# Moving 128 value loads from SyncE's to GpSimd's queue, with a new step order, in a local attention and MLP kernel

## The chip, the cores and the metric

The kernel runs on one core of a Trainium2 chip. The metric is the device time of one execution in microseconds (us). Before the change, three runs took 199.34, 200.52 and 202.75 us; the median is 200.52. Names of engines: PE is TensorE, DVE is VectorE, ACT is ScalarE, POOL is GpSimd, SP is SyncE. SP computes nothing; its queue issues DMA transfers. POOL computes a little and can issue transfers too.

## The reference

The input `x` has 2048 rows (positions) of 512. It is normalised by rows, and the result `xn` goes through two branches that are multiplied and, with `x`, make the output `x + s * g`, in the kernel's terms.

```python
xn = _layernorm(x)
# branch A: local attention, 32 heads of 16, 8 keys per query at distance 0, 2, ... 14
q, k, v = split(xn @ wqkv)
idx = pos[:, None] - off[None, :]          # off = 0, 2, ..., 14
logits = einsum("bhsd,bhswd->bhsw", q, k[idx]) * scale
logits = where(idx >= 0, logits, -1e9)     # the mask: only the first 14 rows have it
s = einsum("bhsw,bhswd->bhsd", softmax(logits), v[idx]) @ wo
# branch B: a shifted mixer and an MLP
h  = gelu(_layernorm(xn) @ w1)
x1 = xn + shift_groups(h) @ w2             # four groups of columns, shifted by 1, -1, 2, -2 rows
g  = silu(x1 + gelu(_layernorm(x1) @ w3) @ w4)
return x + s * g
```

## The kernel before, in words

The 2048 rows are 16 tiles of 128 rows, in 4 chunks of 4 tiles. The kernel defines named steps (functions that issue a few instructions) and then runs through one written list, `ORDER`, that calls each step once. An engine executes its own instructions in that order and each instruction waits for its inputs, so the list fixes five queues, one per engine, that proceed at their own pace. The number in a name is a tile (0 to 15) or a chunk (0 to 3); `lv3.0` is part 0 of the load of tile 3, `qk1.2` part 2 of chunk 1.

The steps that the change and the prediction touch:

- `x0`..`x3`, `xc1`..`xc3` load `x`. `st` (L262) takes the statistics on DVE; `rsa`, `rsb`, `rsc`, `r2a`, `r2b` turn them into scales (`rsb` L275 and `r2b` L297 on POOL); `xn` normalises (L304 on DVE in chunk 0, L308 on ACT after it).
- `tr0`..`tr3` (L329) transpose the tiles of chunk 0 on PE into one PSUM tile of two banks, `xe0`..`xe3` (L334) copy them out on ACT. Chunk 1 is transposed by PE and copied by DVE (`tr1.0`, `xe1.0`), chunks 2 and 3 by DMA from SP (`tx`, L339).
- `qk` (L393) makes eight blocks of q and k for a chunk, `qe` (L399) copies them out on ACT. `v` and `h` (L405) make the values and the mixer's input for one tile; `ve` (L411) copies the values to an SBUF tile of which there are three, and `vst` (L416) stores them to DRAM from POOL's queue. `he` (L420) applies the gelu on ACT, `hst` (L426) transposes by DMA from SP into `hT`.
- `pw` (L448) multiplies q with shifted k on DVE, `lg` (L457) sums over each head on PE. For chunk 0 `mask` (L464) writes -1e9 into the logits. Then `mx`, `ls`, `to`, `sh` (DVE) and `ex` (ACT) make the softmax of a chunk, `et` (L506) transposes it on PE, `ae` (L512) copies it out.
- `lv` (L655) loads the eight shifted copies of the values of a tile back from DRAM into one of three `vs` buffers, four DMAs per step. `pr` (L661) multiplies them by the weights in place on DVE, `ws` (L670) sums on PE, `oe` (L676) copies out, `oTe` transposes (by DMA from SP, L690; for the last three tiles by PE in `ot`), `wo` (L715) multiplies by the output weights. A `vs` buffer is free again when its `ws` is done.
- `mix` (L553) is the shifted product with `w2`: it needs the `hT` of its own tile and of its neighbours, and at the ends of a chunk the columns that `pl` and `pr_` (L540, L547) copy on POOL. `xo` (L559), `s3` (L562), `ra3`, `rb3` (L571, POOL), `rc3`, `xm` (L580, ACT) normalise; `x1T` (L586) transposes by DMA from SP; `w3` (L608), `ge` (L615), `w4` (L623), `yy` (L629), `si` (L632) are the MLP; `sg` (L720), `fa` (L723) and `out` (L727) combine and store.

Every DMA of this kernel waits, besides its data, for the transfer eight places before it on the same kind of queue, since eight semaphores go round. Matmul results go through six PSUM buffers; a matmul step waits until the step six places before it has been copied out.

Of the kernel before, what the change touches and what calls it, by code (L numbers as in the profile page):

```python
# [16 lines left out]
warm0 sel x1 qa0 x0 x2 w1 x3 root wqk0 wqk1 st0 wv st1 xc1 rsa0 w2 xn0 rsa1 st2 tr0 xe0 xn1 rsa2 st3 wo.0 h0  # L17
xn2 rsa3 tr1 xn3 tr2 xe1 xe2 tr3 r2a0 h1 xe3 r2q0 h2 r2b0 he0 h3 v0 he2 hst0 qk0.6 ve0 st6 he1 qk0.0 vst0 w3.1
st7 qe0.6 pl0 hst1 v2 qe0.0 st4 qk0.3 ve2 st5 hst2 vst2 he3 rsa1.0 qe0.3 rsb1.0 lv0.0 v1 qk0.5 ve1 rsc1.0 r2a1
xn6 qk0.2 vst1 hst3 qe0.5 r2b1 qk0.1 xn4 xc3 qe0.2 mix1 lv0.1 qe0.1 qk0.7 xn5 xo1 xn7 qk0.4 s31 xc2 qe0.7  # L20
tr1.0 qe0.4 lv1.0 tr1.1 xe1.0 mix0 qa1 pw0.0 h4 xe1.1 lv1.1 v5 he4 xo0 qk1.2 st12 ve5 qk1.7 vst5 s30 hst4
qe1.2 st11 lg0.0 qe1.7 qk1.0 lv2.0 pl1 st8 h7 qe1.0 st10 qk1.4 w4.1 he7 st9 qk1.5 lv2.1 pw0.2 qe1.4 pr_0 h5
qe1.5 rsa2.0 st14 rsb2.0 qk1.6 he5 hst7 st15 v3 qe1.6 rsc2.0 hst5 st13 xn8 mix2 r2a2 ve3 v4 tx8 rsa3.0 xn10
r2b2 pw0.1 mix3 xn9 tx10 xo2 rsb3.0 ve4 v7 xo3 xn11 qk1.1 vst4 s32 tx9 ve7 vst3 rsc3.0 qk1.3 r2a3 qe1.1 vst7
w3.0 s33 xn15 lg0.2 r2b3 tx11 lg0.1 pw0.7 qe1.3 h6 xn12 mix4 ra30 he6 pw0.5 rb30 xn13 h8 hst6 xo4 xn14 v8 rc30
s34 he8 v6 xm2 hst8 h10 ve8 ve6 vst8 tx12 lg0.7 xm0 lg0.5 vst6 pw0.4 v10 he10 pl2 x1T0 xm3 h9 pw0.6 ve10 pr_1
tx13 h11 he9 vst10 lg0.6 he11 lg0.4 tx15 mix5 pw0.3 mix7 x1T2 pw1.0 qa2 v11 tx14 xo7 qk2.7 ve11 xo5 w3.3 qk2.1
vst11 s37 qe2.7 w3.2 v13 s35 qe2.1 hst10 xm1 qk2.3 ve13 x1T3 lg0.3 qe2.3 qk2.2 vst13 mask x1T1 qk2.4 pw1.1
qe2.2 v9 hst11 qe2.4 mx0 mix6 ve9 hst9 ls0 v12 vst9 h14 w4.2 xo6 ve12 ex0 s36 qk2.5 vst12 h12 ra31 rb31 v14
he14 to0 w4.0 lg1.0 h15 rc31 sh0 w30.7 qe2.5 he12 qk2.0 ve14 hst12 he15 pw1.2 w30.4 vst14 ge0.7 pl3 hst14 et0  # L30
qe2.0 pr_3 w30.5 ge0.4 ae0 xm5 hst15 w30.9 pr0 ge0.5 w30.1 xm4 pr_2 ge0.9 qk2.6 x1T4 ge0.1 pr1 xm7 ws0 x1T5
lg1.2 qe2.6 lg1.1 w30.10 oe0 lv3.0 pw1.5 v15 ge0.10 w30.8 pw1.3 ve15 x1T7 w30.3 vst15 ge0.8 pr2 xm6 lg1.3
lg1.5 lv3.1 ge0.3 w30.2 w30.6 ge0.2 pw1.4 x1T6 w30.0 ge0.6 pw1.7 ws2 ge0.0 oTe0 lg1.4 oe2 ws1 pw1.6 lg1.7 w42
lv4.0 pw2.4 qa3 pr3 oTe2 qk3.6 oe1 oTe1 w41 qe3.6 yy2 lv4.1 si2 ws3 yy1 lg1.6 w40 oe3 lv5.0 mx1 si1 pw2.0 oTe3
ls1 mix9 lv5.1 qk3.5 xo9 ex1 yy0 mix10 s39 mix8 lv6.0 xo10 qk3.7 qe3.5 xo8 si0 to1 qk3.4 lv6.1 w31.2 s38 qe3.7
w43 qe3.4 sh1 ge1.2 s310 qk3.1 yy3 et1 qe3.1 w31.8 ae1 si3 w31.6 pr4 w31.4 ge1.8 w31.10 pr5 wo.3 mix11 wo.2
ge1.10 w31.9 ge1.4 ge1.6 w31.7 xo11 ge1.9 wo.1 pr6 ws5 ge1.7 lg2.0 oe5 ws4 lg2.4 oe4 lv7.0 w31.3 pw2.1 wo1
ge1.3 pw2.3 wo0 lv7.1 w31.5 sg1 s311 w31.1 ge1.5 oTe5 fa1 wo2 ra32 ge1.1 sg0 rb32 lv8.0 lg2.3 sg2 lg2.1 w31.0
pw2.6 qk3.0 ge1.0 out1 rc32 pw2.5 oTe4 xm8 h13 qe3.0 pr7 w45 xm11 x1T8 he13 xm9 lv8.1 fa0 wo3 fa2 yy5 lg2.5
x1T9 sg3 si5 lg2.6 qk3.3 pw2.2 hst13 w47 pw2.7 qe3.3 xm10 x1T11 fa3 lg2.2 out3 yy7 lg2.7 out2 ws7 out0 mx2 si7  # L40
ws6 x1T10 qk3.2 oe7 oe6 ls2 w44 oTe7 qe3.2 pw3.2 ex2 oTe6 pw3.0 w46 lv9.0 yy4 to2 si4 lv9.1 mix12 yy6 w32.5
sh2 si6 mix14 lv10.0 ge2.5 w32.8 xo12 xo14 et2 ge2.8 lv10.1 w32.1 s312 ae2 w32.10 ge2.1 s314 mix15 ge2.10 pr8
w32.6 mix13 ge2.6 w32.7 xo15 xo13 wo6 ge2.7 s315 wo5 s313 w32.0 sg5 lg3.0 ra33 sg6 ge2.0 ws8 rb33 lg3.2 pr10
oe8 lv11.0 w32.2 w32.4 ge2.2 w32.9 oTe8 rc33 ge2.4 pr9 xm12 w32.3 lv11.1 ge2.9 wo7 xm14 pw3.4 wo4 ge2.3 xm13
x1T12 w411 sg7 sg4 x1T14 pw3.5 x1T13 ws10 fa5 yy11 lg3.5 oe10 lg3.4 w48 pr11 si11 out5 oTe10 xm15 pw3.7 w49
x1T15 yy8 pw3.1 si8 lg3.7 fa4 ws9 pw3.6 out4 lg3.1 oe9 w410 lv12.0 fa7 pw3.3 oTe9 yy9 lg3.6 yy10 lg3.3 si9
# [10 lines left out]
def kernel(  # L57
# [202 lines left out]
    def plan_ln1(c, t, dk):  # L260
# [63 lines left out]
        def tr1(i):  # L324
            if i == 0:
                ps["tr0"] = ps_lg.tile([P, 2, 2, ND, P], BF16, name="tr0_ps", tag="lg")
            pt = ps["tr0"][:, i % 2, i // 2, :, :]
            for dt in range(ND):
                nc.tensor.transpose(pt[:, dt, :], xn_t[i][:, dt * P : (dt + 1) * P], ident[:])  # L329

        def xe1(i):
            if i == 0:
                xnT_t[0] = xnTp.tile([P, ND, CH], BF16, name="xnT", tag="xnT")
            nc.scalar.activation(xnT_t[0][:, :, i * P : (i + 1) * P], ps["tr0"][:, i % 2, i // 2, :, :], AF.Copy)  # L334
# [311 lines left out]
    def plan_attend(i, t, tw):  # L646
        c, jj = i // TPC, i % TPC

        def load_vs(uh):
            if uh == 0:  # L650
                vs_t[i] = vsp.tile([P, NB, 2, D], BF16, name="vs", tag="vs")
            vs = vs_t[i]
            for u in range(U4 * uh, U4 * uh + U4):
# [1 line left out]
                nc.sync.dma_start(  # L655
                    out=vs[T32 * (u % U4) : T32 * (u % U4) + T32, :, u // U4, :],
                    in_=v_dram[r0 : r0 + P, :].rearrange("(b t) d -> t b d", t=T32))
# [142 lines left out]
```

## Time and profile before

| what | value |
|---|---|
| median of 3 runs | 200.52 us |
| the profiled execution | 202.74 us |
| its span, first to last instruction | 201.0 us |
| mean granted PE clock | 0.989 |
| PE busy | 187.4 us, 93% |
| DVE busy | 165.6 us, 82% |
| ACT busy | 132.5 us, 66% |
| POOL busy | 30.8 us, 15% |
| transfers on SP's queue (q1) | 33.24 MB, 67.8% of the 16 DMA engines' span |
| transfers on POOL's queue (q0) | 2.11 MB, 3.2% |

In the profile's lines a group reads: line, engine, operation, output tile <- input tiles, shapes, count, then the busy time in us and the mean duration in ns, then the idle time of the engine just before, with what ended it. In the table of 40 slices each digit is the busy share of one fortieth of the span (5.0 us) in tenths; PEclk is the granted clock in tenths. A line of waits reads: who waited, for whom, total us, how often, the longest. In a timeline a line begins with its start and its length in us; "x4" means that four instructions are shown as one. "SPq" is SP's queue issuing transfers, which is not counted as busy.

### The profile page before, as it was taken

The page shows a single profiled execution, that of the slowest core. Times are in us where ns is not written, and L with a number is a line of the kernel's source. Part 1 is how long each engine was busy: PE and PEld are TensorE (multiplying, and loading weights), DVE is VectorE, ACT ScalarE, POOL GpSimd, SP SyncE. Part 2 cuts the span into 40 slices and gives each one's busy share as a digit, 9 for nine tenths or more (in the row PEclk, how much of TensorE's full clock was granted, in tenths as well). Part 3 has the DMA queues.
Part 4 walks back from the last instruction along what each step waited for, and adds up shares of the span by engine and source line. Part 5 has one row for each costly group of instructions (what it writes and reads, how often), then busy time and mean ns, then how long its engine had stood idle before and what let it go on. Part 6 is the DMA issues. An engine that isn't in the chain of part 4 may idle for free.

```text
span 201.0 us, 3994 instructions
## 1 busy us (share of the span) xinstructions
PE 187.4 (93%) x1470; PEld 90.0 (45%) x1496; DVE 165.6 (82%) x265; ACT 132.5 (66%) x204; POOL 30.8 (15%) x48
## 2 busy tenths in 40 slices
PE   7599999939999999999999999999999999999991
PEld 7344544413444444454444444445444444444440
DVE  5752667993496799997999999899999999689854
ACT  3498856595837799727689639497446629953370
POOL 4015220692731411120000020000020000000000
PEclk9999999996999999999999999999999999999999
DMA  5988999999699654766985446666937567798302
GB/s 186 343 260 188 256 248 256 253 141 243 153 108 258 165 169 95 203 144 179 224 215 139 116 126 181 176 116 172 252 76 203 129 138 186 215 258 248 93 29 79
DMA packets 57908, 36.27 MB, mean 180 GB/s; under 512 B 31794, under 2 KB 56864, under 8 KB 57888
## 3 DMA queue, kind: packets, MB, share of 16 engines
q1 hardware_dynamic: 56416, 33.24, 67.8%
q0 software_dynamic: 800, 2.11, 3.2%
q10 hardware_dynamic: 672, 0.66, 1.0%
q8 instruction: 12, 0.20, 0.4%
q14 instruction: 8, 0.07, 0.2%
HBM read 24.84 MB, written 4.21 MB: 145 GB/s over the span
## 4 chain that ended last, share of the span: by engine, by line
PE 86%; DMA 4%; ACT 4%; DVE 3%; issue 1%; ACTq 0%; DVEq 0%
PE w_ps L608 19%; PE w_ps L623 19%; PE qk_ps L393 13%; PE v_ps L405 7%; PE w_ps L553 6%; PE h_ps L405 6%; PE wo_ps L715 6%; PE lg L457 4%; PE o_ps L670 4%; DMA xnT<-xn 3%; DMA x_all<-in_A_x_dram 1%; DVE stats L262 1%; PE et_ps L506 1%; ACT vct L411 1%; ACT xn L308 1%
## 5 line engine op out<-in xcount | busy, mean ns | idle before, releaser
L448 DVE TENSOR_TENSOR pw<-qT,kT 128x2048 bf16<-128x2048 bf16 x32 | 38.2, 1216 | 5.3 <-PE lg L457 5.1
L608 PE MATMUL w_ps<-x1nT,w_sb 128*128 128x512 bf16 (+1 forms) x168 | 41.1, 380 | 0.4
L623 PE MATMUL w_ps<-w_sb,h3t 128*128 128x512 bf16 (+1 forms) x171 | 39.4, 379 | 0.5 <-issue 0.3
L661 DVE TENSOR_TENSOR vs<-vs,att 128x4096 bf16<-128x4096 bf16 x16 | 36.3, 2287 | 0.2
L615 ACT ACTIVATE h3t<-w_ps 128x512 bf16<-128x512 f32 (+1 forms) x44 | 25.1, 605 | 12.9 <-PE w_ps L608 12.6
L393 PE MATMUL qk_ps<-xnT,wqk_sb 128*128 128x512 bf16 x122 | 30.4, 379 | 0.5 <-issue 0.3
L623 PEld LDWEIGHTS <-h3t 128*128 128x128 bf16 (+1 forms) x176 | 16.7, 98 | 20.7 <-issue 0.8
L608 PEld LDWEIGHTS <-w_sb 128*128 128x128 bf16 (+1 forms) x176 | 16.9, 100 | 19.1 <-DMA vs<-v_dram 0.4
L405 PEld LDWEIGHTS <-xnT 128*128 128x128 bf16 x128 | 12.6, 101 | 16.8 <-issue 2.3
L553 PE MATMUL w_ps<-w_sb,hT 128*128 128x512 bf16 x63 | 16.2, 379 | 3.6 <-DMA hT<-ht 3.6
L393 PEld LDWEIGHTS <-wqk_sb 128*128 128x128 bf16 x128 | 12.2, 98 | 14.9 <-issue 0.4
L676 ACT ACTIVATE o_sb<-o_ps 128x512 bf16<-128x512 f32 x16 | 9.5, 598 | 12.8 <-DMA oT<-o_sb 3.7
L405 PE MATMUL v_ps<-wv_sb,xnT 128*128 128x512 bf16 x62 | 17.2, 398 | 0.1
L405 PE MATMUL h_ps<-w_sb,xnT 128*128 128x512 bf16 x61 | 16.0, 393 | 1.0 <-ACT xnT L334 0.7
L632 ACT ACTIVATE g<-g 128x512 bf16<-128x512 bf16 x16 | 10.0, 629 | 10.1 <-DVE g L629 10.0
L262 DVE BATCH_NORM_STATS2 stats<-x_all 128x6 f32<-128x512 bf16 x16 | 10.8, 675 | 4.7 <-DMA x_all<-in_A_x_dram 4.7
L715 PE MATMUL wo_ps<-wo_sb,oT 128*128 128x512 bf16 x59 | 14.5, 379 | 0.2
L416 POOL DMA_DIRECT2D v_dram<-vct x16 | 9.0, 563 | 36.5 <-ACT vct L411 36.5
L420 ACT ACTIVATE ht<-h_ps,rstd 128x512 bf16<-128x512 f32 x16 | 10.9, 687 | 5.0 <-issue 2.0
L571 POOL TENSOR_TENSOR rstd<-ve,mhalf 128x4 f32<-128x4 f32 x4 | 4.3, 1067 | 58.4 <-DVE ve L566 58.4
L580 ACT ACTIVATE xn<-x,nmr,rstd 128x512 bf16<-128x512 bf16 x16 | 13.1, 819 | 0.0
L629 DVE TENSOR_TENSOR g<-w_ps,x 128x512 bf16<-128x512 f32 x16 | 10.7, 681 | 2.8 <-PE w_ps L623 2.8
(84 smaller groups left out, 234.0 us busy)
## 6 DMA issues: line engine op xcount, KB each, us to landing
vs<-v_dram SPq DMA_DIRECT2D x128, 128.0 KB, 3.0
v_dram<-vct POOLq DMA_DIRECT2D x16, 128.0 KB, 2.9
out_dram<-x_all SPq DMA_DIRECT2D x15, 128.0 KB, 2.5
x_all<-in_A_x_dram SPq DMA_DIRECT2D x3, 512.0 KB, 7.0
...
```

The costliest lines, as they stand in the source:

```text
L262: nc.vector.bn_stats(out=stats1[:, i, :], in_=x_all[:, i, :])
L393: nc.tensor.matmul(pt, lhsT=wqk_sb[:, dt, nt * P : (nt + 1) * P], rhs=xnT_t[c][:, dt, :], start=(dt == 0), stop=(dt == ND - 1))
L405: nc.tensor.matmul(pt, lhsT=xnT_t[c][:, dt, jj * P : (jj + 1) * P], rhs=w_sb[:, dt, :], start=(dt == 0), stop=(dt == ND - 1))
L420: nc.scalar.activation(ht_t[i], ps.pop(f"h{i}"), AF.Gelu_apprx_tanh, scale=rstd2[:, i : i + 1])
L448: nc.vector.tensor_tensor(out=pw, in0=q_t[c], in1=k_t[c][:, :, DIL * u : DIL * u + CH], op=ALU.mult)
L553: nc.tensor.matmul(pt, lhsT=hT_t[c][:, g, b0 + shift[g] : b0 + shift[g] + P], rhs=w2_sb[:, g, :], start=(g == 0), stop=(g == ND - 1))
L580: nc.scalar.activation(xn3_t[i], x1_t[i], AF.Identity, bias=nmr3[:, i : i + 1], scale=rstd3[:, i : i + 1])
L608: nc.tensor.matmul(pt[:fs, :], lhsT=w3_sb[:, dt, ft * P : ft * P + fs], rhs=x1nT_t[c][:, dt, :], start=(dt == 0), stop=(dt == ND - 1))
L615: nc.scalar.activation(h3_t[c, ft][:fs, :], ps.pop(f"w3{c}.{ft}")[:fs, :], AF.Gelu_apprx_tanh)
L623: nc.tensor.matmul(pt, lhsT=h3_t[c, ft][:fs, jj * P : (jj + 1) * P], rhs=w4_sb[:fs, ft, :], start=(ft == 0), stop=(ft == NF - 1))
L661: nc.vector.tensor_tensor(out=vv, in0=vv, in1=at_t[c][:, :, jj, :].unsqueeze(2).to_broadcast([P, NB * 2, DH, H]), op=ALU.mult)
L715: nc.tensor.matmul(pt, lhsT=oT[:, dt, :], rhs=wo_sb[:, dt, :], start=(dt == 0), stop=(dt == ND - 1))
```

## The change

Four things change. The 128 value loads, four to a step on SP's queue, become 128 steps of one load each on POOL's queue. The mask of chunk 0, seven clears of parts of the logits on DVE, becomes one addition of a constant tile `maskb` that POOL fills at the start. The transposes `tr0`..`tr3` used the two halves of each of two banks; now tiles 2 and 3 write where tiles 0 and 1 were, so still two banks in turn, but a half of each. And `ORDER` is written anew throughout.

```diff
+    maskb = const.tile([P, W, PADK], F32, name="maskb")
...
+    nc.gpsimd.memset(maskb[:], 0.0)
+    for u in range(W - 1):
+        nc.gpsimd.memset(maskb[0:T32, u, 0 : PADK - DIL * u], -1e9)
...
         def tr1(i):
...
-            pt = ps["tr0"][:, i % 2, i // 2, :, :]
+            pt = ps["tr0"][:, i % 2, 0, :, :]
...
         def mask():
-            for u in range(W - 1):
-                nc.vector.memset(lg_t[c][0:32, u, 0 : PADK - DIL * u], -1e9)
+            nc.vector.tensor_tensor(
+                out=lg_t[c][:, :, 0:PADK], in0=lg_t[c][:, :, 0:PADK], in1=maskb[:], op=ALU.add)
...
-        def load_vs(uh):
-            if uh == 0:
+        def load_vs(u):
+            if u == 0:
                 vs_t[i] = vsp.tile([P, NB, 2, D], BF16, name="vs", tag="vs")
-            vs = vs_t[i]
-            for u in range(U4 * uh, U4 * uh + U4):
-                r0 = i * P + DIL * u
-                nc.sync.dma_start(
-                    out=vs[T32 * (u % U4) : T32 * (u % U4) + T32, :, u // U4, :],
-                    in_=v_dram[r0 : r0 + P, :].rearrange("(b t) d -> t b d", t=T32))
+            r0 = i * P + DIL * u
+            nc.gpsimd.dma_start(
+                out=vs_t[i][T32 * (u % U4) : T32 * (u % U4) + T32, :, u // U4, :],
+                in_=v_dram[r0 : r0 + P, :].rearrange("(b t) d -> t b d", t=T32))
...
-        for uh in range(2):
-            add(f"lv{i}.{uh}", lambda uh=uh: load_vs(uh))
+        for u in range(W):
+            add(f"lv{i}.{u}", lambda u=u: load_vs(u))
```

Of the two lists, the stretches that the prediction speaks of (before, then after):

```diff
 the head
-... st2 tr0 xe0 xn1 rsa2 st3 wo.0 h0
-xn2 rsa3 tr1 xn3 tr2 xe1 xe2 tr3 r2a0 h1 xe3 r2q0 h2 r2b0 he0 h3 v0 he2 hst0 qk0.6 ...
+... st2 tr0 xe0 xn1 rsa2 h0 st3 xn2
+tr1 rsa3 xe1 xn3 tr2 xe2 tr3 r2a0 h1 xe3 r2q0 h2 r2b0 he0 h3 v0 v1 hst0 ve0 he2 he1 ve1 he3 vst0 xc2 ...
 around mix4
-... st8 h7 qe1.0 st10 qk1.4 w4.1 he7 st9 qk1.5 lv2.1 pw0.2 qe1.4 pr_0 h5
-qe1.5 rsa2.0 st14 rsb2.0 qk1.6 he5 hst7 st15 v3 qe1.6 rsc2.0 hst5 st13 xn8 mix2 r2a2 ve3 v4 tx8 ...
-w3.0 s33 xn15 lg0.2 r2b3 tx11 lg0.1 pw0.7 qe1.3 h6 xn12 mix4 ...
+he7 qe1.4 ve7 qe1.1 xn11 lg0.6 lg0.7 st12 xo3 pw0.3 pw0.4 tx8 hst5 tx9 tx10 tx11 hst6 hst7 w3.2 qk1.6 qk1.2 v6
+qk1.5 qk1.7 lg0.4 lg0.3 lv1.6 r2b2 lv1.7 vst7 vst4 lv2.0 lv2.1 qe1.2 ve6 qe1.6 qe1.5 qe1.7 st13 s30 s33 mask
+st15 mx0 ra30 ls0 qk1.3 h8 qk1.0 mix4 mix5 mix6 he8 ...
 the first weighted values
-... ae0 xm5 hst15 w30.9 pr0 ge0.5 w30.1 xm4 pr_2 ge0.9 qk2.6 x1T4 ge0.1 pr1 xm7 ws0 x1T5
-lg1.2 qe2.6 lg1.1 w30.10 oe0 lv3.0 ...
+... ae0 xo7 pr0 h11 h9 v8 qk2.4 qk2.1 x1T2
+w4.1 lg1.0 ws0 lg1.5 he11 he9 qe2.4 ve8 qe2.1 lv2.5 lv2.6 lv2.7 rsb3.0 s37 rsc3.0 r2a3 pr1 pw1.1 pw1.4 qk2.6
+w30.8 w30.5 lv3.0 lv3.1 lv3.2 lv3.3 lv3.4 vst5 lv3.5 lv3.6 lv3.7 ge0.8 ...
 the end
-out9 w415 lv15.1 pr14 out11 w414 oTe12 yy15 yy12 si15 ws14 yy14 ws13 si12 pr15 w413 oe14 oe13 si14 ot14 yy13
-wo12 oTe14 si13 ws15 sg12 ot13 oe15 wo14 fa12 oTe13 out12 ot15 sg14 wo13 oTe15 fa14 wo15.0 sg13 out14 wo15.1
-sg15.0 fa13 out15.0 sg15.1 out13 out15.1
+w413 fa11 fa5 pr14 fa8 sg10 pr15 fa10 yy15 sg9 yy12 yy13 oTe13 out4 oTe12 ws15 ws14 wo13 oe15 ot15 si15 si13
+si12 oe14 oTe15 sg13 fa13 fa9 w414 wo15.1 wo15.0 ot14 yy14 sg15.1 wo12 sg15.0 oTe14 si14 wo14 sg12 fa12 sg14
+out3 out8 out10 out6 out9 out11 out1 out0 out15.1 out13 out15.0 out12 out5 fa14 out14
```

More of the change, by code (lines that the diff above doesn't have):

```diff
@@ L16 @@
 ORDER = """
[L17 to L46, printed above, removed]
@@ L52 @@
-sg15.0 fa13 out15.0 sg15.1 out13 out15.1
+warm0 sel x1 x0 qa0 x2 w1 x3 root wqk0 wqk1 wv st0 xc1 st1 w2 rsa0 xn0 rsa1 st2 tr0 xe0 xn1 rsa2 h0 st3 xn2
+tr1 rsa3 xe1 xn3 tr2 xe2 tr3 r2a0 h1 xe3 r2q0 h2 r2b0 he0 h3 v0 v1 hst0 ve0 he2 he1 ve1 he3 vst0 xc2 wo.1 hst1
+hst2 hst3 w4.2 xc3 w4.0 st4 st5 st7 st6 rsa1.0 qk0.0 qk0.5 qk0.3 qk0.1 rsb1.0 pl0 lv0.0 vst1 lv0.1 lv0.2 lv0.3
+rsc1.0 r2a1 st10 st11 st8 st9 rsa2.0 r2b1 lv0.4 rsb2.0 lv0.5 lv0.6 lv0.7 qe0.3 qe0.5 qe0.1 qe0.0 xn7 xn4 xn5
+qk0.6 qk0.2 qk0.4 qk0.7 v3 tr1.0 qe0.6 qe0.2 qe0.7 qe0.4 ve3 xn6 xe1.0 pw0.0 pw0.5 mix0 mix2 h4 tr1.1 lg0.0 v2
@@ new lines @@
+lg0.5 mix1 he4 hst4 w3.3 xe1.1 xo0 rsc2.0 xo2 pw0.2 xo1 pw0.1 s32 s31 r2a2 h5 h6 v4 h7 lg0.1 lg0.2 ve2 xn8 xn9
+he5 he6 lv1.0 qa1 lv1.1 lv1.2 lv1.3 pr_0 lv1.4 vst3 lv1.5 vst2 pl1 pw0.6 pw0.7 qk1.4 v7 mix3 qk1.1 xn10 ve4
+he7 qe1.4 ve7 qe1.1 xn11 lg0.6 lg0.7 st12 xo3 pw0.3 pw0.4 tx8 hst5 tx9 tx10 tx11 hst6 hst7 w3.2 qk1.6 qk1.2 v6
+qk1.5 qk1.7 lg0.4 lg0.3 lv1.6 r2b2 lv1.7 vst7 vst4 lv2.0 lv2.1 qe1.2 ve6 qe1.6 qe1.5 qe1.7 st13 s30 s33 mask
+st15 mx0 ra30 ls0 qk1.3 h8 qk1.0 mix4 mix5 mix6 he8 qe1.3 qe1.0 ex0 hst8 vst6 lv2.2 qa2 lv2.3 rb30 lv2.4 pr_1
@@ new lines @@
+st14 rc30 xo5 xo4 xo6 pw1.0 to0 rsa3.0 sh0 pw1.5 v5 qk2.2 qk2.7 xm0 ve5 qe2.7 xm3 qe2.2 xm1 qk2.0 v10 qk2.3
+mix7 qk2.5 et0 x1T0 w3.0 w3.1 wo.3 x1T1 x1T3 ve10 qe2.3 qe2.0 qe2.5 xm2 ae0 xo7 pr0 h11 h9 v8 qk2.4 qk2.1 x1T2
+w4.1 lg1.0 ws0 lg1.5 he11 he9 qe2.4 ve8 qe2.1 lv2.5 lv2.6 lv2.7 rsb3.0 s37 rsc3.0 r2a3 pr1 pw1.1 pw1.4 qk2.6
+w30.8 w30.5 lv3.0 lv3.1 lv3.2 lv3.3 lv3.4 vst5 lv3.5 lv3.6 lv3.7 ge0.8 qe2.6 oe0 xn12 xn14 xn15 ge0.5 w30.1
+w30.2 w30.6 lg1.4 ws1 lg1.1 w30.4 h10 oe1 ge0.1 ge0.6 ge0.2 he10 ge0.4 pr2 s34 pw1.3 pw1.7 pr3 v11 w30.7 w30.0
@@ new lines @@
+lv9.2 lv9.3 lv9.4 vst15 pl3 lv9.5 rb32 lv9.6 lv9.7 pr7 sg1 pw3.0 to2 rc32 sh2 pw3.3 ge1.5 ge1.10 xm8 ge1.6
+ge1.1 ve14 oTe5 x1T8 w31.7 wo2 v12 v13 et2 lg3.0 ws7 lg3.3 sg2 pw3.7 fa2 ae2 pr8 fa0 pr9 pw3.1 fa3 ge1.7 xm10
+ve13 oe7 xm11 ve12 xm9 hst13 hst14 hst15 oTe6 x1T11 out2 x1T9 oTe7 x1T10 w44 w47 w46 w45 ws9 ws8 lg3.7 lg3.1
+yy7 yy6 yy4 pw3.4 yy5 lv10.0 lv10.1 lv10.2 lv10.3 lv10.4 lv10.5 lv10.6 vst13 lv10.7 lv11.0 lv11.1 si7 si6 oe9
+si5 oe8 si4 mix15 mix14 wo4 mix13 xo15 pw3.6 xo14 sg4 xo13 w32.8 mix12 w32.4 w32.1 w32.3 w32.2 lg3.4 lg3.6
@@ L333, in xe1 @@
                 xnT_t[0] = xnTp.tile([P, ND, CH], BF16, name="xnT", tag="xnT")
-            nc.scalar.activation(xnT_t[0][:, :, i * P : (i + 1) * P], ps["tr0"][:, i % 2, i // 2, :, :], AF.Copy)
+            nc.scalar.activation(xnT_t[0][:, :, i * P : (i + 1) * P], ps["tr0"][:, i % 2, 0, :, :], AF.Copy)
         def tx(i):
```

21 lines of the change are left out of this document (18 added, 3 removed).

## The prediction

> **What bounds the kernel now.** I read the busy shares first, then the 40 slices, then the waits of TensorE (PE), then the timeline around the longest of them.
>
> ```profile
> PE 187.4 (93%) x1470; PEld 90.0 (45%) x1496; DVE 165.6 (82%) x265; ACT 132.5 (66%) x204; POOL 30.8 (15%) x48
> ...
> PE   7599999939999999999999999999999999999991
> ...
> PEclk9999999996999999999999999999999999999999
> DMA  5988999999699654766985446666937567798302
> ```
>
> PE is busy 187.4 of 201.0 us, so at most 13.6 us of idle time can go. The digits below 9 say where it lies: the head, one hole in slices 9 and 10 (40 to 50 us, where the granted clock drops too), and the tail. The chain that ended last agrees: 86% of it is PE.
>
> ```profile
> PE w_ps L553 <- DMA hT<-ht: 3.6, 1, 3.6
> PE warm_ps L250 <- POOL ident masks.py:199: 1.4, 1, 1.4
> PE tr_ps L329 <- ACT xnT L334: 1.2, 1, 1.2
> ```
>
> The hole is one wait of 3.6 us: the matmuls of step mix4 (L553) for a transposed `hT`. Why that came late, SyncE's (SP's) queue tells:
>
> ```profile
> 33.03 1.95 SPq L655 DMA_DIRECT2D vs<-v_dram  x4
> 35.02 0.43 SPq L214 DMA_DIRECT2D w_sb<-in_B_w_dram  x1
> 35.50 1.96 SPq L655 DMA_DIRECT2D vs<-v_dram  x4
> 37.55 3.27 SPq L426 DMA_TRANSPOSE hT<-ht  x2
> ```
>
> ScalarE finishes the activation he5 (L420) at 33.86. Its transpose hst5 is the second at 37.55: it stood behind eight value loads, a weight load and another transpose, and landed only at 45.4. What follows the hole:
>
> ```profile
> 46.39 1.75 PE L405 MATMUL h_ps<-w_sb,xnT 128*128 128x512 bf16 x4 [0.17 <-DMA xnT<-xn]
> 47.94 2.90 PE L405 MATMUL v_ps<-wv_sb,xnT 128*128 128x512 bf16 x7
> 50.68 1.03 PE L405 MATMUL h_ps<-w_sb,xnT 128*128 128x512 bf16 x4
> ```
>
> Four such matmuls take 1.03 us at 50.68 and 1.75 at 46.39. In the chain the slow stretch costs 0.9 us over the h matmuls and 1.0 over the first five v: 1.9 in all. So the hole is worth 3.6 + 1.9 = 5.5 us.
>
> **The change, part by part.** The profiled execution took 202.74 us (span 201.0 and 1.7 around it), 2.2 above the 200.52 median of three runs. I sum against 202.74 and take the difference from the median.
>
> *Loads leave SP's queue.* SP loses 128 issues of about 0.49 us (1.95 for four), 62 us. What stays is 53 transposes at about 1.2 us and some 35 plain transfers. In the new order he5 ends near 31.3 us (ScalarE's L399, L308, L411 and L420 ahead of it at their row means, from the 24.7 us reached below). hst5 then has only tx8 before it and is issued near 32.5. mix4 comes two PE us later in the order, near 44.5. Even the slowest landing of this group (7.3 us) is in time. Gain: 5.5. What is late next is hst7, behind tx9, tx10, tx11 and hst6: xn11 ends near 37.9, so hst7 is issued near 41.5. With a landing of 3.2 (median) to 7.3 us it is there between 44.7 and 48.8; mix6 wants it at 46.3. I charge 1.0.
>
> *Loads enter POOL's queue.* No load of this shape (32 partitions by 4 by 512) is issued there in this trace. The nearest row is L416, stores of the same 128 KB:
>
> ```profile
> L416 POOL DMA_DIRECT2D v_dram<-vct x16 | 9.0, 563 | 36.5 <-ACT vct L411 36.5
> ...
> vs<-v_dram SPq DMA_DIRECT2D x128, 128.0 KB, 3.0
> v_dram<-vct POOLq DMA_DIRECT2D x16, 128.0 KB, 2.9
> ```
>
> I take 0.56 us per issue and 2.9 us to landing. POOL is then busy 128 x 0.56 + 30.8 = 103 us of some 195. The lower end is SP's 0.49. The upper end comes from a POOL operation that VectorE (DVE) holds up:
>
> ```profile
> 38.72 1.22 DVE L448 TENSOR_TENSOR pw<-qT,kT 128x2048 bf16<-128x2048 bf16 x1
> ...
> 72.85 1.22 DVE L448 TENSOR_TENSOR pw<-qT,kT 128x2048 bf16<-128x2048 bf16 x1
> ```
>
> ```profile
> 38.82 1.98 POOL L297 TENSOR_TENSOR rstd<-ve,mhalf 128x4 f32<-128x4 f32 x1 [1.87 <-DVE ve L270]
> 40.78 1.00 POOL L275 TENSOR_TENSOR rstd<-ve,mhalf 128x4 f32<-128x4 f32 x1
> ...
> 73.30 0.60 POOL L416 DMA_DIRECT2D v_dram<-vct  x1 [3.97 <-ACT vct L411]
> ```
>
> Inside a DVE product POOL's arithmetic took 1.98 instead of 1.0. A DMA issue inside one took 0.60, against 0.54 at best. The store is nearer to the load than the arithmetic is, so 0.56 stands; the upper end is 0.56 + 0.95 = 1.5. The Trainium skill (SBUF — State Buffer, Who interferes with whom) speaks against this move: descriptors for POOL's DMAs are written over ports shared with DVE and starve while DVE runs a two-port copy, cast or tensor_scalar, whereas a tensor_tensor with two SBUF inputs only stops a POOL operation that reads. By that rule the pw and pr products cost the loads nothing; the two rows at 38.82 and 73.30 agree.
>
> Behind a load that waits, POOL now also holds the stores of v (whose buffers ScalarE waits for), the rstd powers (L275, L297, L571) and the pads. The tightest case I find: lv3.0 waits for ws0, near 59 us. Eight loads and one store at 0.56 plus 2.9 are 7.9 us, and DVE reaches pr3 some 10 us after ws0 (its rows between: s37, pr1, two pw, pr2, s34, two more pw). Cost 0, with 2 us to spare. lv0.0 waits for the first store to land (14.6 + 2.9); nothing urgent stands behind it. rsb2.0 waits near 24.7 for the statistics of chunk 2, but vst3 behind it is wanted only near 35. Cost 0; if that cover goes, ve7 on ScalarE is late one for one.
>
> *Head.* Before, tr3 waited until both copies xe1 and xe2 were done (9.74). In the new order each copy waits for its own transpose and tr3 only for xe1, so it starts near 8.7: 1.1 us gained. Its lower bound is 0, if the same bank is still held.
>
> *Mask.* Seven clears (0.78 us with the product that lies between them not counted) become one addition of 112 elements: from 682 ns at 512 and 415 at 256 elements (L720, L702), about 0.27. DVE gains 0.5 off the path. The eight clears of `maskb` on POOL lie before 4 us, where POOL has nothing due until 14.6. Cost 0.
>
> *The rest of the order.* Around 13 us of PE work moves from ahead of ws0 to behind it, so DVE's large products (36.3 us at L661) start near 56 instead of 75 us. DVE then runs closer ahead of PE. Walking the row means: q and k of chunk 0 are evacuated by 24.7 (24.3 before); qk0.1 waits 0.6 for a PSUM buffer that he3 frees; lg0.1 waits 0.4 for pw0.1; et0 and ws0 find their inputs with 1 to 2 us to spare. I charge 1.0 for the two waits. ScalarE's table loads go from 19 to 16 (3 x 1.28 us), off the path. The tail: before, 9.65 us pass from the last w4 matmul (191.35) to the end. Now five DVE pieces (0.6 to 0.75) with a final sum (0.4) and one store (2.5) follow the last w4, some 7 us; but 2 us of PE work also move ahead of it. I take 0.5, between 0 and 1. Several stores of earlier tiles now stand late in SP's queue at 0.43 each; that is hidden by DVE's last 4 us.
>
> **Sum:** 5.5 + 1.1 + 0.5 - 1.0 - 1.0 = 5.1, so 197.6 against 202.74, and 200.5 - 5.1 = 195.4 for the median; **195.4**, 2.5% less. With all idle time but the first 1.4, 2 at the head and 4.4 at the tail gone it could gain 7.7: 192.8, the floor.
>
> **Rivals.** *A: the hole is only filled in another way.* From 20 to 50 us the windows give the 16 DMA engines a busy share of 0.99, 1.00 and 1.25, so transfers are late whoever issues them, and DVE's thin lead at et0 and ws0 may turn into waits. Against: hst5 alone waited about 5 us before it was issued. With the hole kept and the head gained: 199.4. The Trainium skill (DMA: Bandwidth & Descriptors, Issuing engines are not separate DMA queues) says that issuing from another engine saves only the sequencer's time, since all share the 16 engines. By that rule the 6.5 us from issue to landing of hst5 would stay, and this is the result.
>
> *B: POOL's queue becomes the bound, slower.* Its place is the stretch from ws0 on, where every tile's eight loads wait for a buffer. From 59 to about 184 us twelve tiles follow, 10.4 each; POOL's other work there is about 1.1 per tile. So the queue decides from (10.4 - 1.1) / 8 = 1.16 us per load. At 1.25, between my value and the upper end, it loses 12 x 8 x 0.09 = 8.6 us, and pr3 is 4.5 late: about 207. Against: the row at 73.30, and three stores back to back in 1.67 us. For: thin evidence, and another shape.
>
> *C: the move does nothing,* since the loads wait for buffers, not for a queue; only the order counts. It ends within A's times and I count it there.
>
> **How the numbers follow.** Forecast 0.53 (192.8 to 198.5), A with C 0.22 (198 to 202), B 0.25 (203 to 220). A measurement here can tell about 2% from no change: below 196.5 is faster, above 204.5 slower. Of the forecast I put 0.43 of its 0.53 below 196.5, with 0.02 from A. B gives 0.24 above 204.5. The range reaches from 192.5 to 207.
>
> **What would show it.** Right: no PE wait for `hT` over 1 us between 40 and 50, granted clock full there, loads at 0.5 to 0.6 us on POOL, first pr near 56 us. Wrong: loads over 0.75 us, DVE waiting at the vs product for DMA, or PE waiting at et and ws for DVE. The forecast fails if the load's shape costs POOL twice the store's time, or if the reordered start opens a hole of its own.

## The result, and the profile after

The changed kernel took 213.41 us (median of four runs, 210.48 to 214.50) where the kernel before took 200.60. The ratio is 1.054, with a 95% interval from 1.046 to 1.062: 5.4% slower, where 2.5% faster was forecast. The profiled execution took 210.48 us, with a span of 208.6, against 202.74 and 201.0 before. (A run that lies more than 1.5% above the fastest one of its own kernel is left out of the ratios given here; the traces of before (202.74, fastest run 199.34), "before, loads on POOL", "stores first" and "first three tiles on SP" come from such runs, so they are read for where a wait stands, not for a few tenths.) The medians differ by 12.8 us and the two profiled executions by 7.7, since the one of after is its fastest: the traces account for the 7.7 and say nothing of the rest.

The page of the kernel after, busy shares and the table of slices:

```profile
PE 190.3 (91%) x1496; PEld 91.5 (44%) x1496; DVE 165.2 (79%) x259; ACT 125.9 (60%) x201; POOL 101.2 (49%) x184
...
PE   7699999749799999999998999999999983999991
...
PEclk9999999966999999999999999999999999999998
DMA  5969999959985899999599962797544999755124
```

PE is busy 190.3 us instead of 187.4, and idle 18.3 of its span instead of 13.6: 2.9 and 4.7 make the 7.6 us by which the two spans differ (26 of the 1496 matmuls are missing from the trace of before, so a part of the 2.9 may be theirs). One hole stands where it stood before, in slices 8 to 11, now with two slices of a low clock, not one. There is a second one, in slices 33 and 34 (171 to 177 us), that the kernel before did not have. The waits of PE name both (waiter, what it waited for, us in total, times, longest):

```profile
PE qk_ps L402 <- ACT vct L420: 4.3, 1, 4.3
PE w_ps L617 <- issue: 3.9, 1, 3.9
PE w_ps L562 <- DMA hT<-ht: 1.5, 1, 1.5
...
PE w_ps L617 <- DMA x1nT<-xn: 1.0, 1, 1.0
```

Before, only the wait of 3.6 us for `hT` was of this size. The four waits here make 10.7.

The first hole, in the chain that ended last, in order of time (start, us, what; only the steps that matter):

```profile
26.35 6.48 DMA hT<-ht
...
32.88 0.24 POOL hT L556
...
34.49 9.26 DMA v_dram<-vct
...
43.83 0.60 ACT vct L420
```

The store in this chain is `vst3`. ScalarE had its data ready at 23.87 (`ve3`), but in POOL's queue it stood behind nine loads, three small operations and the pad `pr_0` (L556), which held POOL for 1.2 us until a transpose of `hT` landed, 6.5 us after its issue. So it is issued at 34.49, and it lands 9.3 us later. Only then is there a `vct` buffer for `ve7` on ScalarE, which had been free since 34.13. Of its wait of 9.7 us, 3.3 would be there with a landing of 2.9 us too; the other 6.4 are the landing. Behind `ve7` PE stands still:

```profile
39.84 0.38 PE L402 MATMUL qk_ps<-xnT,wqk_sb 128*128 128x512 bf16 x1
44.48 1.86 PE L402 MATMUL qk_ps<-xnT,wqk_sb 128*128 128x512 bf16 x4 [4.27 <-ACT vct L420]
...
48.93 1.79 PE L414 MATMUL h_ps<-w_sb,xnT 128*128 128x512 bf16 x4
50.56 1.03 PE L402 MATMUL qk_ps<-xnT,wqk_sb 128*128 128x512 bf16 x4
...
54.13 1.86 PE L562 MATMUL w_ps<-w_sb,hT 128*128 128x512 bf16 x7 [1.47 <-DMA hT<-ht]
...
175.38 1.89 PE L617 MATMUL w_ps<-x1nT,w_sb 128*128 128x512 bf16 x8 [3.86 <-issue]
```

Four matmuls take 1.8 us up to 50.5 and 1.03 after it, so the slow clock follows the hole as it did before. The wait at 175.38 is put down to "issue", that is, to nothing that the chain shows. The view of the tile `x1nT` shows it: its transposes of this stretch are issued between 157.6 and 165.1, and the last of them takes the longest to land, 10.2 us; 165.1 + 10.2 = 175.3, where PE goes on.

What both holes have in common is in the issues of DMA. The page of after (issues with their median us to landing; queues with packets, MB, share of the 16 engines; and the costliest group on POOL):

```profile
q0 software_dynamic: 6944, 18.90, 41.6%
q1 hardware_dynamic: 37984, 16.46, 38.8%
...
L662 POOL DMA_DIRECT2D vs<-v_dram x128 | 70.4, 555 | 54.5 <-PE o_ps L677 22.9
...
vs<-v_dram POOLq DMA_DIRECT2D x128, 128.0 KB, 4.7
v_dram<-vct POOLq DMA_DIRECT2D x16, 128.0 KB, 4.4
```

A load costs POOL 0.555 us, as forecast. But it lands after 4.7 us instead of 3.0, and the stores of v, which were on POOL all along, after 4.4 instead of 2.9. The transposes, which never left SP's queue, are later too. Landing in us, minimum, median and maximum of each tile's transposes:

| transposes on SP | before | after |
|---|---|---|
| `hT` | 2.3 / 3.2 / 7.3 | 2.5 / 5.0 / 10.5 |
| `xnT` | 2.4 / 3.5 / 5.4 | 6.0 / 8.6 / 10.9 |
| `x1nT` | 2.3 / 2.6 / 4.8 | 2.4 / 3.9 / 10.2 |
| `oT` | 2.3 / 2.5 / 4.8 | 2.4 / 5.8 / 13.0 |

This is not more traffic. In the window from 110 to 190 us the kernel before moves 169 GB/s and the one after 157, yet (issues of that window, before):

```profile
vs<-v_dram SPq DMA_DIRECT2D x72, 128.0 KB, 3.0
oT<-o_sb SPq DMA_TRANSPOSE x9, 2.4
x1nT<-xn SPq DMA_TRANSPOSE x8, 2.4
```

and after:

```profile
vs<-v_dram POOLq DMA_DIRECT2D x63, 128.0 KB, 4.2
...
oT<-o_sb SPq DMA_TRANSPOSE x8, 5.4
x1nT<-xn SPq DMA_TRANSPOSE x8, 5.3
```

SP has far less to issue and its transposes take twice as long to land.

### The profile page after: what moved, and what is told of

Its sections match the earlier page's. It is cut to its first block, busy times and chain, and to the rows that moved or that the text cites. A ratio compares the mean times of both kernels' runs of the same rounds, so it can differ in the third digit from the quotient of the medians.

```text
span 208.6 us, 4030 instructions
## 1 busy us (share of the span) xinstructions
PE 190.3 (91%) x1496; PEld 91.5 (44%) x1496; DVE 165.2 (79%) x259; ACT 125.9 (60%) x201; POOL 101.2 (49%) x184
## 4 chain that ended last, share of the span: by engine, by line
PE 68%; DMA 21%; DVE 4%; issue 3%; ACT 2%; SPq 0%; POOL 0%; ACTq 0%
PE w_ps L617 19%; PE w_ps L632 14%; PE qk_ps L402 10%; DMA x1nT<-xn 7%; DMA hT<-ht 7%; PE wo_ps L722 5%; PE v_ps L414 5%; PE w_ps L562 5%; DMA v_dram<-vct 4%; PE h_ps L414 4%; PE o_ps L677 3%; PE lg L466 3%; DMA x_all<-in_A_x_dram 1%; DVE stats L271 1%; DMA oT<-o_sb 1%
## 5 line engine op out<-in xcount | busy, mean ns | idle before, releaser
L662 POOL DMA_DIRECT2D vs<-v_dram x128 | 70.4, 555 | 54.5 <-PE o_ps L677 22.9
L617 PE MATMUL w_ps<-x1nT,w_sb 128*128 128x512 bf16 (+1 forms) x176 | 40.5, 379 | 4.8 <-issue 3.9
L402 PE MATMUL qk_ps<-xnT,wqk_sb 128*128 128x512 bf16 x128 | 32.3, 395 | 4.3 <-ACT vct L420 4.3
L624 ACT ACTIVATE h3t<-w_ps 128x512 bf16<-128x512 f32 (+1 forms) x44 | 24.2, 595 | 19.1 <-PE w_ps L617 18.9
L727 DVE TENSOR_TENSOR g<-wo_ps,g 128x512 bf16<-128x512 f32 x15 | 10.2, 684 | 12.0 <-ACT g L641 8.0
L420 ACT ACTIVATE vct<-v_ps 128x512 bf16<-128x512 f32 x16 | 9.6, 600 | 13.4 <-DMA v_dram<-vct 9.7
L414 PE MATMUL h_ps<-w_sb,xnT 128*128 128x512 bf16 x64 | 16.6, 393 | 0.7 <-ACT xnT L343 0.7
L414 PE MATMUL v_ps<-wv_sb,xnT 128*128 128x512 bf16 x64 | 16.1, 379 | 0.0
L589 ACT ACTIVATE xn<-x,nmr,rstd 128x512 bf16<-128x512 bf16 x16 | 12.8, 808 | 5.1 <-DVE nmr L583 4.0
```

The source lines that it names most:

```text
L402: nc.tensor.matmul(pt, lhsT=wqk_sb[:, dt, nt * P : (nt + 1) * P], rhs=xnT_t[c][:, dt, :], start=(dt == 0), stop=(dt == ND - 1))
L414: nc.tensor.matmul(pt, lhsT=xnT_t[c][:, dt, jj * P : (jj + 1) * P], rhs=w_sb[:, dt, :], start=(dt == 0), stop=(dt == ND - 1))
L589: nc.scalar.activation(xn3_t[i], x1_t[i], AF.Identity, bias=nmr3[:, i : i + 1], scale=rstd3[:, i : i + 1])
L617: nc.tensor.matmul(pt[:fs, :], lhsT=w3_sb[:, dt, ft * P : ft * P + fs], rhs=x1nT_t[c][:, dt, :], start=(dt == 0), stop=(dt == ND - 1))
L624: nc.scalar.activation(h3_t[c, ft][:fs, :], ps.pop(f"w3{c}.{ft}")[:fs, :], AF.Gelu_apprx_tanh)
L662: nc.gpsimd.dma_start(out=vs_t[i][T32 * (u % U4) : T32 * (u % U4) + T32, :, u // U4, :], in_=v_dram[r0 : r0 + P, :].rearrange("(b t) d -> ...
```

## The theories and the experiments

The expectations below use these letters. **D**: loads issued from POOL make the other transfers, SP's transposes above all, land later. **Q**: POOL's queue itself, executed in order, holds urgent small steps (`pr_0`, `vst3`) behind steps that wait. **O**: the new order alone, whichever queue issues the loads. In the table, the experiments down to "tile 2's loads later" ran on one chip (before: 200.51 us there), the three below on another (before: 202.71). The times are medians of all runs.

| kernel | us | ratio to before, 95% interval | landing of `hT`, `x1nT`, `xnT`, `oT`, loads (medians) |
|---|---|---|---|
| before | | 1 | 3.2, 2.6, 3.5, 2.5, 3.0 |
| after | 213.41 | 1.054 (1.046 to 1.062) | 5.0, 3.9, 8.6, 5.8, 4.7 |
| after, loads back on SP | 202.99 | 1.015 (1.005 to 1.024) | 3.5, 3.2, 3.1, 3.3, 4.0 |
| before, loads on POOL | 202.98 | 1.014 (1.004 to 1.023) | 3.6, 4.2, 3.7, 6.0, 5.1 |
| after, stores first | 218.64 | 1.083 (1.073 to 1.092) | 5.5, 5.2, 11.1, 5.6, 5.7 |
| before, tile 2's loads later | 204.45 | 1.024 (1.019 to 1.030) | 3.4, 2.5, 2.7, 2.6, 3.1 |
| before, tile 2's loads much later | 199.84 | 0.985 (0.979 to 0.990) | 3.2, 2.8, 2.9, 2.7, 3.2 |
| after, first three tiles on SP | 206.30 | 1.014 (1.005 to 1.023) | 4.7, 5.0, 6.1, 6.4, 5.1 (POOL), 5.0 (SP) |
| after, loads of half the bytes | 205.77 | 1.012 (1.005 to 1.019) | 4.0, 2.9, 4.7, 3.8, 3.1 |

**After, with the loads back on SP**: the change without its move.

```diff
-            nc.gpsimd.dma_start(
+            nc.sync.dma_start(
```

> The changed kernel with its new order, mask and transposes, only the 128 single loads issued from SP's queue again. Three theories for the 13 us lost. Q (POOL's queue: the v stores stand behind loads that wait, a store lands 9.3 us after its issue, ScalarE waits 9.7 us for a value buffer, PE 4.3): gone here, 200 to 204 us. D (the DMA engines: loads issued from POOL take more of them, so transposes land late, xnT 8.6 instead of 3.5 us, oT 5.8 instead of 2.5): landings return to 2.5 to 4 us, 199 to 204 us. O (the new order itself, whatever the queue): stays at 208 us or more, and the landings need not change.

Measured: 1.015. The wait of 4.3 behind `ve7` and the one at 175 are gone; the longest waits of PE for data are 2.8 us in three pieces for `pw` and 1.6 for `hT`. In the window from 110 to 190 us, at 154 GB/s:

```profile
oT<-o_sb SPq DMA_TRANSPOSE x8, 2.9
x1nT<-xn SPq DMA_TRANSPOSE x8, 2.5
```

So the queue of the loads, and not the order, makes the transposes late. The order alone is 1.5% slower than the old one (interval 0.5% to 2.4%).

**Before, with the loads on POOL**: the move without the order, four loads to a step as before.

```diff
-                nc.sync.dma_start(
+                nc.gpsimd.dma_start(
```

> The kernel before with its old order, only the 128 loads issued from POOL's queue, in the same steps of four. Q: the old order was not written for it, so stores, powers and pads wait behind loads: 207 us or more, with waits of ScalarE for value buffers. D: transposes land late as in the changed kernel (xnT over 6, oT over 5 us median), 205 to 212 us. O: 196 to 201 us, since SP's queue is relieved and the order is the old one; landings as before.

Measured: 1.014. From 110 to 190 us `oT` lands after 5.6 and `x1nT` after 5.2, at 164 GB/s, as in the kernel after. PE's one long wait here is

```profile
PE w_ps L553 <- POOL hT L547: 3.8, 1, 3.8
```

that is, for a pad that POOL issues: the old hole for `hT` is gone and one behind POOL stands in its place. So for `oT` and `x1nT` D holds in both orders. The time is below D's 205 to 212 all the same, and `xnT`, expected over 6, lands after 3.7. The two parts, 1.5% and 1.4%, do not add up to 5.4%: some 2.5% exists only where both are together, by the three intervals between about 1% and 4%.

**After, with each store right behind the copy that fills it**, ahead of the loads and pads that it stood behind.

```diff
-... v0 v1 hst0 ve0 he2 he1 ve1 he3 vst0 xc2 ... pl0 lv0.0 vst1 lv0.1 ... pr_0 lv1.4 vst3 lv1.5 vst2 ...
+... v0 v1 hst0 ve0 vst0 he2 he1 ve1 vst1 he3 xc2 ... pl0 lv0.0 lv0.1 ... v3 ... ve3 vst3 ... ve2 vst2 ...
```

> The changed kernel, with each store of v moved in the written order to directly behind the copy that makes it, so ahead of loads on POOL's queue. Q: ScalarE's wait of 9.7 us and PE's hole at 40 us go, 5 to 8 us are won: 203 to 206 us. D: stores leave earlier but loads and transposes still land late, and the hole before w3 of the last chunk (3.9 us) stays: 207 to 211 us. O: no change, 211 to 214 us.

Measured: 1.083, worse than the change itself and than any of the three theories had it. The stall of ScalarE for a store is gone (0.6 us are left of 9.7). But now nothing pauses: between 31 and 45 us POOL issues nine loads where it issued five in after, and SP five transposes for two. `xnT` lands after 11.1 us (8.6 in after), and the hole comes back as a wait for `hst6`, which is issued at 42.76 and lands after 13.3 us:

```profile
PE w_ps L562 <- DMA hT<-ht: 8.9, 1, 8.9
PE w_ps L617 <- issue: 4.3, 1, 4.3
```

So Q says through which step the lateness reached PE; its remedy does not remove the lateness. Both lines are waits for SP's transposes, the second as at 175 us in after.

**Before, with tile 2's eight loads moved behind `hst6`**: is the old hole made by SP's queue, as the prediction said?

```diff
-... qk1.0 lv2.0 pl1 st8 ... qk1.5 lv2.1 pw0.2 ...
+... qk1.0 pl1 st8 ... qk1.5 pw0.2 ...
...
-... h8 hst6 xo4 xn14 ...
+... h8 hst6 lv2.0 lv2.1 xo4 xn14 ...
```

> The kernel before, with only the eight loads of tile 2 moved in the written order from ahead of the transposes hst7 and hst5 to behind hst6 (all on SP). If the hole of 3.6 us at 41.8 and the slow clock after it came from SP's queue, as the prediction says, it closes: 194.5 to 197 us. If transfers are late there whoever is ahead, the transposes land no earlier: 199 to 201 us.

Measured: 1.024, 204.45 us where 194.5 to 197 were expected if the hole closed. No wait of PE for a transfer is left between 37 and 50 us, but there is a new one. SP's queue and PE (timeline):

```profile
46.37 3.92 SPq L655 DMA_DIRECT2D vs<-v_dram  x8
50.39 1.23 SPq L426 DMA_TRANSPOSE hT<-ht  x1
...
55.96 1.46 PE L553 MATMUL w_ps<-w_sb,hT 128*128 128x512 bf16 x3 [4.13 <-POOL hT L547]
```

The eight loads now stand ahead of `hst8`; the pad `pr_1` waits for it and PE for the pad. The hole moved with the loads, as it does if SP's queue makes it.

**Before, with the same loads behind `w4.0`**, past `hst8` too and close to their use.

```diff
-... qk1.0 lv2.0 pl1 st8 ... qk1.5 lv2.1 pw0.2 ...
+... qk1.0 pl1 st8 ... qk1.5 pw0.2 ...
...
-he14 to0 w4.0 lg1.0 ...
+he14 to0 w4.0 lv2.0 lv2.1 lg1.0 ...
```

> The kernel before (all loads on SP, old order), with the eight loads of tile 2 moved to behind the weight load w4.0, so that hst7, hst5, hst6 and hst8 all have fewer loads ahead on SP. The last run closed the hole at 41.8 us but opened one of 4.1 us at 52, where the pad copy waits for hst8, which then stood behind those loads. If both holes are SP's queue: 195 to 198 us. If a hole only moves on to the next transpose, since transfers are late in this stretch whatever is ahead: 200 to 203 us.

Measured: 199.84 against 202.71, 0.985 with an interval from 0.979 to 0.990. This one beats both kernels. Its slices, and the queue of SP where `hst7` and `hst5` are issued:

```profile
PE   7699999999899999988999999999999999999991
PEclk9999999999999999999999999999999999999998
```

```profile
34.69 2.51 SPq L426 DMA_TRANSPOSE hT<-ht  x2
```

The pair starts at 34.69 instead of 37.55, no wait for `hT` is left, and the clock stays full (0.996). What PE waits for longest now is 1.5 us for a `vs` product on DVE. Its loads are issued when they were (from 83.3 us, before from 83.1), but the first products now start 4.0 us earlier (71.0 for 75.0), and DVE waits 3.2 us for the loads.

**After, with the loads of tiles 0 to 2 on SP** and the other 104 on POOL.

```diff
-            nc.gpsimd.dma_start(
+            (nc.sync if i < 3 else nc.gpsimd).dma_start(
```

> The changed kernel with the loads of tiles 0 to 2 on SP, those of tiles 3 to 15 on POOL. D (loads from POOL make transposes land late): the first stretch recovers, xnT of chunk 2 lands in about 3 us, the hole at 40 us and its slow clock (some 8 us) go, but oT and x1T of the later tiles still land in 4 to 6 us and the hole before w3 of chunk 3 stays: 203 to 207 us. Q (stores behind loads in POOL's order): the first hole goes too, but landings late in the kernel have no reason to stay long: oT near 3 us, 200 to 203 us.

Measured: 1.014. The hole near 40 us is gone, the one in w3 stays:

```profile
PE w_ps L617 <- issue: 4.1, 1, 4.1
PE w_ps L617 <- DMA x1nT<-xn: 2.4, 1, 2.4
```

and so do the late landings (`oT` 6.4, `x1nT` 5.0). The `xnT` of chunk 2 lands after 3.0 to 5.7 us, where about 3 were expected, and that of chunk 3, when POOL has the loads, after 6.5 to 9.6. So the two holes of after are separate, and each goes when the loads near it leave POOL's queue or shrink (the next kernel).

**After, with half the bytes in each load**: as many issues on POOL, in the same order.

```diff
-                out=vs_t[i][T32 * (u % U4) : T32 * (u % U4) + T32, :, u // U4, :],
-                in_=v_dram[r0 : r0 + P, :].rearrange("(b t) d -> t b d", t=T32))
+                out=vs_t[i][T32 * (u % U4) : T32 * (u % U4) + T32, :, u // U4, 0 : D // 2],
+                in_=v_dram[r0 : r0 + P, 0 : D // 2].rearrange("(b t) d -> t b d", t=T32))
```

> The changed kernel, same queues, order and number of loads, but each load brings only the first half of the columns (64 of 128 KB; the other half of three fixed buffers is filled with zeros by POOL before 12 us, so half of the weighted values are zero). D, if bytes in flight make the transposes late: their landings fall towards 3 to 4 us and 6 to 10 us are won: 201 to 206 us. Q, if POOL's waiting order does it: no change in the waits for stores, 209 to 213 us.

Measured: 1.012, although the zeros that POOL writes from 3.0 to 8.4 us hold up DVE (its first statistics take 5.0 us instead of 0.7) and add a wait of their own:

```profile
PE tr_ps L341 <- DVE xn L316: 4.7, 1, 4.7
...
PE w_ps L620 <- DMA x1nT<-xn: 1.1, 1, 1.1
...
PE w_ps L565 <- DMA hT<-ht: 0.6, 2, 0.4
```

Both holes of after are gone with POOL's issues unchanged (0.548 us each); the stores land after 2.9 us again. The bytes that POOL's queue carries made the holes, not the time that POOL spends to issue. That disposes of Q as a cause by itself.

**Landing by itself**: transfers only. Eight transposes from SP, alone, beside 16 loads from POOL, from ScalarE, and from SP between the transposes.

```diff
+    last = phase(nc.gpsimd, 0, last)
+    last = phase(nc.gpsimd, 2, last)
+    last = phase(nc.scalar, 2, last)
+    last = phase(nc.sync, 2, last)
```

> No part of the reference's computation: only transfers, in eight stretches that follow one another. In each, eight transposes of 128 by 512 are issued from SP, (a) alone, (b) beside 16 value loads issued from POOL, (c) beside 16 from ScalarE's queue, (d) with two from SP ahead of each; then the same four again. D with large packets (a load takes 48 packets on POOL's queue, 144 on SP's, and a transpose's small packets wait for one at each turn): (a) 2.3 us to landing, (b) 5 to 7, (c) 3 to 4, (d) 3 to 4. If any second queue does it, whatever its packets: (c) like (b). If it takes the rest of the kernel: (b) below 3.5.

Measured in one execution, two rounds, median landing of a transpose: alone 2.5 and 2.5 us; beside loads from POOL 9.0 and 9.0; from ScalarE 4.5 and 4.3; from SP itself 2.7 and 2.6. So (b) came out above its 5 to 7, (c) a little above and (d) below their 3 to 4. The loads of the first round landed after 8.1, 3.4 and 2.6. (POOL's loads began a stage early in each round, since their buffers were free, beside the transposes meant to run alone, and the next eight ran alone in their place; the figures go by what ran together, five transposes in the first round. In the next kernel all are let go together.) In the stretch beside POOL (issues of the window from 20.5 to 39 us):

```profile
vs<-v_dram POOLq DMA_DIRECT2D x15, 128.0 KB, 8.6
tt<-src SPq DMA_TRANSPOSE x5, 9.0
```

This is D with no kernel around it. One possible reason is in the packets. A load of 128 KB takes 48 packets on POOL's queue (6144 for 128 in the kernel after, 2.7 KB each) and 144 on SP's or ScalarE's; a transpose takes 544, all under 512 bytes, 34 for each of the 16 engines. The Trainium skill (DMA: Bandwidth & Descriptors, Queues, rings and completion order) says that each DMA engine goes round the queues packet by packet. By that rule a transfer of many small packets waits at each for a large one of the other queue. The last kernel tried this.

**The same with three forms of transfer on SP**, all of 128 KB: rows of 1 KB (`tk`, 9 packets an engine), rows of 256 bytes (`tt`, 33) and transposes (`tr`, 34), each alone, beside 24 loads from POOL and beside 24 from ScalarE, let go together.

```diff
+    for kind in "kqt":
+        last = phase(kind, nc.gpsimd, 0, last)
+        last = phase(kind, nc.gpsimd, 3, last)
+        last = phase(kind, nc.scalar, 3, last)
```

> Transfers alone, no computation of the reference (its output is a copy of x rows, so its total time means nothing). Eight transfers of 128 KB from SyncE's queue, of three forms: k, a copy in rows of 1 KB; q, the same copy in rows of 256 bytes; t, the transpose. Each form runs alone, then beside 24 value loads issued from GpSimd's queue, then beside the same 24 from ScalarE's, all let go at the same moment; twice over. Theory P (the 16 DMA engines take packets from the queues in turn, and the packet of a load on GpSimd's queue is 4 KB, on ScalarE's 1 KB, so what counts is how many packets the other transfer has on each engine): beside GpSimd's loads k, with about 8 packets on an engine, is later by 8 x 0.25 = 2 us, q and t, with 32 to 37, by 7 to 9 us; beside ScalarE's loads k by 0.5 to 1, q and t by about 2. Rival M (the engines share by bytes, or the loads merely fill them): all three forms carry the same 128 KB and are late by the same 2 to 4 us. Rival T (something about the transpose itself, not about packets): k and q stay within 2 us of their time alone, t alone goes to 7 or more.

Measured in one execution, median landing in us, first and second round:

| on SP | alone | beside POOL's loads | beside ScalarE's loads |
|---|---|---|---|
| rows of 1 KB | 2.1, 2.1 | 6.5, 7.3 | 2.8, 2.8 |
| rows of 256 bytes | 2.3, 2.3 | 7.8, 8.2 | 4.0, 4.1 |
| transposes | 2.5, 2.5 | 8.5, 10.4 | 3.5, 3.5 |

T falls: plain copies suffer like transposes. P falls as a sum: with 9 packets on an engine, 2 us more were expected and 4.4 to 5.2 were measured, and four times the packets added only 0.7 to 2.7 us to that. (What falls is P's sum; that the engines go round the queues packet by packet may be so all the same.) What stands is that loads from POOL's queue delay whatever SP issues by 4.4 to 7.9 us, and the same loads from ScalarE's queue by 0.7 to 1.8.

M, that the loads merely fill the engines, is not refuted by this, for the two queues did not put the same bytes beside the eight transfers. Every DMA waits for the one eight places before it on the same kind of queue, and in this trace ScalarE's loads take the same eight semaphores in turn as SP's transfers, while POOL's have eight of their own. So with ScalarE at most 8 transfers were out (issued and not landed) at a time, with POOL up to 15. From the first to the last issue of the eight transposes of the first round (issues of the windows from 134.1 to 145.1 us and from 164.2 to 173.8):

```profile
vs<-v_dram POOLq DMA_DIRECT2D x16, 128.0 KB, 6.8
tr<-src SPq DMA_TRANSPOSE x8, 8.5
...
vs<-v_dram ACTq DMA_DIRECT2D x7, 128.0 KB, 2.8
tr<-src SPq DMA_TRANSPOSE x8, 3.5
```

Sixteen loads went out beside the transposes from POOL, seven from ScalarE. All 32 transfers together took not much longer with POOL: 19.6 to 27.0 us, against 18.9 to 24.6. Loads issued while 4 to 7 other transfers were out landed alike, after 4.0 us from POOL and 3.9 from ScalarE; 8 or more were out only beside POOL, and then they took 6.9. In the kernels, too, more were out where landings were late: 4.0 on average and 10 at most in before, 4.6 and 9 in after with the loads back on SP, 5.5 and 13 in before with the loads on POOL, at least that in after. (These counts are worked out from the issues and landings in the traces.) So the likeliest reason is M: POOL's loads come on top of the eight that SP may have out, and all share one rate. It is argued, not shown: a late landing raises the count by itself, SP's own transfers issued at an equal count are too few to compare (four of each form beside POOL, and these are later than beside ScalarE), and no run held the count fixed.

## Why the prediction was wrong, point by point

**The diagnosis of the kernel before held.** The hole at 41.8 us was made by loads standing ahead of `hst5` in SP's queue: moving eight of them a little moves the hole, moving them further closes it, and the clock stays full. Two things go together there: `hst5` is issued 2.9 us sooner (35.98 for 38.84) and lands after 5.6 us instead of 6.5. That its place in the queue was not all of it, the chain of before shows, which passes the hole through another transpose:

```profile
40.93 5.42 DMA xnT<-xn
```

It was issued as soon as ScalarE had its input, and landed at 46.35, 1.0 us after `hst5`. The worth was taken too high: 5.5 us by the sum, 2.9 us measured (202.71 less 199.84), which the new wait of 1.5 us for DVE has made smaller.

**POOL's issue price held.** 0.56 us was taken and 0.555 measured (128 issues, 0.550 to 0.602, with DVE busy 79% of the span); POOL was to be busy 103 us and is 101. Rival B, which needed 1.16 us, fell with it. On this point the rule of the Trainium skill that was weighed (SBUF — State Buffer, Who interferes with whom) agrees: two-input products did not starve the issues.

**The step that failed is the landing.** "I take 0.56 us per issue and 2.9 us to landing" took the landing from stores that ran while all the loads were on SP. The loads took 4.7 and the stores themselves 4.4. Worse, the sum left the landing of everything else as it was: hst5 was given 7.3 us at the worst and hst7 "3.2 (median) to 7.3", and `hT` came to 5.0 at the median and 10.5 at most, which is hst5 itself, `xnT` to 8.6 at the median. (`hst5` was issued at 30.14, before its forecast 32.5, and so in time even then.) The trace of before had no row of a transpose beside POOL's loads, and I bounded the issue from both sides and the landing not at all.

**The failing landing fell on a cover that was named and priced at nothing.** "vst3 behind it is wanted only near 35 ... if that cover goes, ve7 on ScalarE is late one for one." The store's data were ready at 23.87, and it was issued at 34.49, which is late even for a landing of 2.9 us, since ScalarE stood ready at 34.13: 3.3 us of ScalarE's wait of 9.7 come from the queue that was priced at nothing, 6.4 from the landing at 43.75. PE lost 4.3. What held the store in line was not `rsb2.0` but the loads of two tiles and `pr_0`. That the queue alone was not the cause, the kernel with the stores first shows.

**The hole of before was exchanged, not closed.** The forecast gain of 5.5 and the charge of 1.0 for `hst7` became waits of 4.3, 1.5 (for `hT`, up to 54.13), 1.0 and 3.9, all behind a late landing. The 1.5 follow from the 4.3: the last `xnT` transpose of the chunk waited for ScalarE, and behind it hst6 was issued at 46.91 and hst7 at 48.22, where the forecast for hst7 was 41.5. The wait in w3 at 175 us is in a stretch of which the prediction said nothing.

**The small terms.** Head: 1.1 expected, nothing came, the lower bound; `tr3` starts at 9.96 (9.78 before). It does not wait for `xe1` alone, which ends at 8.84: `tr2` starts at 8.88, just after `xe1`, and `tr3` just after `xe2`, which ends at 9.91, so each transpose still waits for the copy before it. Tail: some 7 us after the last w4 expected, 7.1 measured. The new order costs about 1.5% on its own, where 1.0 us was charged for its two waits. The first weighted product starts at 64.6 us where about 56 was expected (75.0 before). Two sums do not come out as written: the idle time left by the floor's own terms is 13.6 less 7.8, so 5.8 and not 7.7 unless the 1.9 of the slow clock is added, and B's losses of 8.6 and 4.5 on 195.4 make 208.5 and not 207. Neither decided anything.

**The rivals.** A came nearest in kind. It held that transfers are late whoever issues them, and drew on the Trainium skill (DMA: Bandwidth & Descriptors, Issuing engines are not separate DMA queues): another issuer saves only the sequencer's time. The runs agree in that nothing but issue time was saved, but by that rule, as A read it, the 6.5 us of hst5 would stay, and they became 10.5. So A's 199.4 was too good, and no rival had transfers that are hurt by the move, with the time that this gives. C, that the move does nothing, is refuted by the two kernels that undo it or do it alone.
